# Two zero products instead of three, the first keys and queries on two queues, the cap behind them

## Chip, core and metric

The kernel runs on one core of one Trainium2 chip. The metric is the device time of one execution in microseconds (us), as the median of several runs. Engines are named as in the profile: PE (TensorE, the products; PEld its weight loads), ACT (ScalarE), DVE (VectorE), POOL (GpSimd) and SP (SyncE, which issues nearly all transfers).

## What is computed

Capped attention (4 batches, 12 heads, 448 positions, 64 values a head), followed by a gated feed-forward layer with a three-tap convolution over the positions:

```python
def _attn_ref(q, k, v, cap):
    scores = np.matmul(q, k.transpose(0, 1, 3, 2)) / np.sqrt(q.shape[-1])
    scores = cap * np.tanh(scores / cap)
    attn = np.exp(scores - np.max(scores, axis=-1, keepdims=True))
    attn = attn / (np.sum(attn, axis=-1, keepdims=True) + 1e-09)
    return np.matmul(attn, v)

def _moe_ref(x, w_in, conv_w, w_out):       # x: (4, 448, 768)
    h = np.maximum(x @ w_in, 0.0)           # (4, 448, 1024)
    ...                                     # conv_out: three taps of conv_w over the positions of h
    return h * (1 / (1 + np.exp(-conv_out))) @ w_out
```

## The kernel before

**Tiles.** Two heads lie together on the 128 partitions as a *pair*, six pairs a batch, 24 in all. `prepare` (L381) loads a pair's keys (`kr`, 128x512), queries (`qr`, 128x448) and values (`vr`, 128x512). `scores` (L420) multiplies a *unit* of 128 keys with all queries, for the two heads side by side on the two halves of the array: three units a pair, plus a rest unit (`spr`) with the last 64 keys of both heads. The first twelve pairs (`RAW`) use f32 operands, which the PE runs as two passes a product. A unit of scores stays in PSUM (`sp`, two buffers), ACT takes the tanh in place (L454, scaled by `tsc_sb`, a factor made from the cap by two DVE operations, L287 and L288) and then the exponential into SBUF (`E`, L458, scaled by `cap_sb`). `values` (L463) multiplies E with the values (`acc`); row sums come from products with ones (`sm`, L572, for the first pairs) or from sums on DVE (`P`). The result is copied out (`su`, `xu`), divided, split into two float parts (`x`) and fed to the feed-forward products `hps` and `ops`.

**Weights.** While the first pairs run, `weight_unit` (L307) turns 64-bit weights into two f32 parts. Each block is one operation on ACT (L322), three on DVE (L324 to L329), a cast to the high part (`wi_h`) and a subtraction (`wi_l`). The cast, as the copies `su`, `xu` and the cast `x`, is made by `either` (L246): it may run on ACT or on DVE.

**Order.** Every step is a `Task` with an engine, an assumed cost, a due time and its predecessors. `Plan.run` (L85) goes through them once, on the host, while the program is built: each engine takes, among the tasks that can start, the one due first, and an `either` task goes to the engine where it would end first by the assumed costs. So a change of a due time or a cost at the start can move later instructions, and can move a copy from one engine to the other. On the chip each engine works through its list in this fixed order.

**The start.** The plan gives these steps the earliest due times. SP loads the cap first (`t_cap`, L265, due -98: 4 bytes copied to each of 128 partitions), then the first pair's keys, queries and values (due -97, -97, -94), then the next ones. DVE fills `ones` and the padded tile `hp[0]` and the borders of two more (`consts`, L267). Then PE runs three products of `ones` with the zero tile (`warm`, L277), whose result nobody reads, and ACT takes an exponential of one column of it (`t_tab`, L284), which brings ACT's function table in. The first scores, on PE behind the warm products, need the first pair's keys and queries; the first tanh needs those scores and `tsc_sb`.

Of the kernel before, what the change touches and what calls it, by code (L numbers as in the profile page):

```python
# [10 lines left out]
ACTF = mybir.ActivationFunctionType  # L11
# [11 lines left out]
STEP = (9.5,) * 8 + (17.2,) * 16  # L23
FIRST = 6.0
DUE = {"w_in": (4.4, 57.93), "w_out": (63.06, 84.72), "prep": -5.0, "load": -34.0, "av": 5.0, "sum": 4.0,
       "x": 14.0, "x0": 14.0, "one": 4.5, "rec": 2.0, "ff": 27.0, "gate": -25.0, "wq": 6.0, "wld": -15.0}
AHEAD = {"w": 20.0, "qk": 40.0, "v": 36.0, "wld": 60.0}
BIAS, SWITCH = {"act": 1.0, "dve": 1.0}, 0.1
SLACK = {"pe": 0.0, "act": 0.1, "dve": 0.1, "sp": 0, "pool": 0}
# [7 lines left out]
HALF = 0.3755  # L37
COLD = (4.0, 0.4, 7.0)
SUMPE = 4
WARM = 3  # L40
LAND = 1.8
GBS = 300.0
RECIP = 2.95
# [129 lines left out]
def capped_attention_gated_mlp_kernel(  # L173
# [50 lines left out]
    plan = Plan({"sp": 2, "acc": 2, "m": 2, "su": 1, "cs": 1, "o": 2, **BUFS})  # L224
    task = plan.task
    ENGINE = {"sp": nc.sync, "pool": nc.gpsimd, "act": nc.scalar}
    ISSUE = {"sp": 0.65, "pool": 1.06, "act": 0.1}

    def f32(ap):
        return ap.bitcast(F32)  # L230
# [1 line left out]
    def dma(queue, nbytes, out, in_, due, deps, take=(), uses=(), after=0.0):  # L232
        def emit():
            a, b = out(), in_()
            ENGINE[queue].dma_start(out=a, in_=b)

        return task(queue, ISSUE[queue], emit, due, deps, take, uses, size=nbytes / (GBS * 1e3), after=after)

# [23 lines left out]
        return FIRST + sum(STEP[:p]) + (STEP[min(p, NP - 1)] * u)  # L262


    t_cap = dma("sp", 512, lambda: cap_sb, lambda: cap.to_broadcast([128, 1]), -98, ())  # L265

    def consts():  # L267
        nc.vector.memset(ones, 1.0)
        nc.vector.memset(ones[half[1], 64:96], 0.0)
        nc.vector.memset(ones[half[0], 96:128], 0.0)  # L270
        nc.vector.memset(hp[0], 0.0)
        for h in hp[1:]:
            nc.vector.memset(h[:, 0:1], 0.0)
            nc.vector.memset(h[:, S + 1:S + 2], 0.0)

    t_const = task("dve", 0.75, consts, -99)
    def warm():  # L277
        t = ps_m.tile([128, 512], F32, tag="m", name="warm")
        for _ in range(WARM):
            nc.tensor.matmul(out=t[:, 0:S], lhsT=ones, rhs=hp[0][:, 0:S], start=True, stop=True)  # L280

    if WARM:
        task("pe", 4.0 / 1.8, warm, -99, [t_const], [Buf("m")])
    t_tab = task("act", 0.1, lambda: nc.scalar.activation(out=eps_sb, in_=hp[0][:, 0:1], func=ACTF.Exp), -99, [t_const])  # L284

    def score_scale():
        nc.vector.reciprocal(out=tsc_sb, in_=cap_sb)  # L287
# [93 lines left out]
    def prepare(p):  # L381
        b, j = divmod(p, NPB)
        t0 = when(p)
        bq, bk, bs = Buf("q"), Buf("k"), Buf("s")
        b_v[p] = Buf("v")
        ld = t0 + DUE["load"] if p else -97
        lk = dma("sp", 128 * KW * 4, lambda: new(p, raw_p, "kr", [128, KW]), lambda: k[b, j], ld, (), [bk],
                 after=t0 - AHEAD["qk"])
        lq = dma("sp", 128 * S * 4, lambda: new(p, raw_p, "qr", [128, S]), lambda: q[b, j], ld, (), [bq],
                 after=t0 - AHEAD["qk"])  # L390
        t_v[p] = dma("sp", 128 * KW * 4, lambda: new(p, raw_p, "vr", [128, KW], bufs=BUFS["v"]), lambda: v[b, j], ld + 3, (),
                     [b_v[p]], after=t0 - AHEAD["v"])
        if p in RAW:
            prep[p], b_in[p] = [lk, lq], [bq, bk]
            return


        due = t0 + DUE["prep"]

        def q_hi():  # L400
            qs = new(p, raw_p, "qs", [128, 2, S], F32R, bufs=BUFS["s"])
            nc.vector.tensor_scalar(out=qs[:, 0], in0=T[p]["qr"], scalar1=tsc_sb[:, 0:1], scalar2=None, op0=ALU.mult)

        def q_lo():
            nc.vector.scalar_tensor_tensor(out=T[p]["qs"][:, 1], in0=T[p]["qr"], scalar=tsc_sb[:, 0:1],
                                           in1=f32(T[p]["qs"][:, 0]), op0=ALU.mult, op1=ALU.subtract)

        def k_hi(eng):
            copy(eng, new(p, raw_p, "ks", [128, 2, KW], F32R, bufs=BUFS["s"])[:, 0], T[p]["kr"])

        def k_lo():
            sub(T[p]["ks"][:, 1], T[p]["kr"], f32(T[p]["ks"][:, 0]))

        a = task("dve", dve(S, one=True, ptr=True), q_hi, due, [lq, t_tsc], [bs], [bq])
        a2 = task("dve", dve(S, ptr=True), q_lo, due + 0.3, [a], uses=[bq, bs])
        c = either(KW, k_hi, due + 0.1, [lk, a], uses=[bk, bs])
        c2 = task("dve", dve(KW), k_lo, due + 0.4, [c], uses=[bk, bs])
        prep[p], b_in[p] = [a, a2, c, c2], [bs]

    def scores(units, due):  # L420

        rest = units[0][1] == NU
        n = 1 if rest else 2
        out = [{} for _ in units]
        bufs = [Buf("m" if rest else "sp") for _ in units]

        def qk():
            for (p, u), sp in zip(units, out):
                if rest:
                    sp[0] = ps_m.tile([128, 512], F32, tag="m", name="spr").rearrange("p (a s) -> p a s", a=1)  # L430
                else:
                    sp[0] = ps_s.tile([128, 2, 512], F32, tag="sp", name="sp")
                X = T[p]
                if p in RAW:
                    parts = [(X["kr"], X["qr"])]
                else:
                    parts = [(X["ks"][:, w], X["qs"][:, l]) for w, l in ((0, 0), (0, 1), (1, 0))]
                for i, (w, x) in enumerate(parts):
                    for h in range(n):
                        r = slice(0, 128) if rest else half[h]  # L440
                        nc.tensor.matmul(out=sp[0][:, h, 0:S], lhsT=w[r, 128 * u:128 * u + 128], rhs=x[r],  # L441
                                         start=i == 0, stop=i == len(parts) - 1)

        cost = sum(2 * HALF if p in RAW else 3 * PASS for p, u in units)
        t_qk = task("pe", cost, qk, due, [t for p, u in units for t in prep[p]], bufs,
                    [b for p, u in units for b in b_in[p]], mode="full" if rest else "row")
        for (p, u), sp, bsp in zip(units, out, bufs):
            t_u = when(p, u / (NU + 1))
            raw = p in RAW
            b_e[p, u] = Buf("e")  # L450

            def tanh(sp=sp, raw=raw):
                x = sp[0][:, 0:n, 0:S]
                nc.scalar.activation(out=x, in_=x, func=ACTF.Tanh, **({"scale": tsc_sb[:, 0:1]} if raw else {}))  # L454

            def exp(p=p, u=u, sp=sp):
                E[p, u] = e_p.tile([128, 2, S], F32, tag="e", name="E")
                nc.scalar.activation(out=E[p, u][:, 0:n], in_=sp[0][:, 0:n, 0:S], func=ACTF.Exp, scale=cap_sb[:, 0:1])  # L458

            t = task("act", act(n * S, True, ptr=raw), tanh, t_u + 1, [t_qk, t_tsc], uses=[bsp])  # L460
            t_exp[p, u] = task("act", act(n * S, True, ptr=True), exp, t_u + 2, [t], [b_e[p, u]], [bsp], table="exp")
# [396 lines left out]
```

## Time and profile before

| | |
|---|---|
| median of 3 runs | 435.05 us (433.42 to 435.63) |
| the profiled execution, its own time | 434.71 us |
| its span, first to last instruction | 432.9 us |
| PE busy | 418.6 us (97%) |
| DVE busy | 309.9 us (72%) |
| ACT busy | 289.1 us (67%) |
| chain that ended last | PE 78%, ACT 11%, DVE 7%, issue 2%, DMA 2% |

The profiled execution's own time is 1.8 us above its span, and 0.34 us below the median of the runs. Busy shares are means over a kernel whose first part (attention of the first pairs, weights) and last part (feed-forward) load the engines quite differently, so the stretches have to be looked at one by one.

### The profile page before, as it was taken

The numbers are of one execution on the slowest core, as the hardware profiler recorded it, in microseconds if no ns is written. First come the engines' busy times: TensorE is split into PE (matmuls) and PEld (weight loads), VectorE is DVE, ScalarE is ACT, GpSimd is POOL, SyncE is SP. The second block draws the span as 40 slices with busy tenths as digits, with TensorE's granted clock in tenths as the row PEclk, the third lists the DMA queues.
The fourth block names the chain that finished last, engine by engine and source line by source line (L and its number), as shares of the span: only waits on it lengthen the run. The fifth ranks groups of instructions, "written<-read, shape, count | busy, mean of one in ns | idle before, by whom it ended". The sixth has DMA issues, their size and how long they took to land.

```text
span 432.9 us, 5890 instructions
## 1 busy us (share of the span) xinstructions
PE 418.6 (97%) x2106; PEld 288.1 (67%) x2106; DVE 309.9 (72%) x548; ACT 289.1 (67%) x412; POOL 0.2 (0%) x4
## 2 busy tenths in 40 slices
PE   7987889999999999999999999999999999999996
PEld 3222234457577676868667868668677787999995
DVE  1788899999999965589899773498899813166400
ACT  4999999988999665358888545368697811454411
POOL 0000000000000000000000000000000000000000
PEclk9999999999999999999999999999999999999999
DMA  7668557887556988650211762633000374500181
GB/s 273 217 225 263 182 181 234 274 244 254 206 161 200 345 292 263 229 210 5 70 28 44 224 225 90 202 130 120 24 2 0 131 251 148 183 0 2 30 336 53
DMA packets 37085, 70.90 MB, mean 164 GB/s; under 512 B 6336, under 2 KB 20160, under 8 KB 37056
## 3 DMA queue, kind: packets, MB, share of 16 engines
q1 hardware_dynamic: 37056, 70.53, 49.8%
q8 instruction: 17, 0.28, 0.3%
q14 instruction: 12, 0.10, 0.1%
HBM read 58.61 MB, written 11.84 MB: 163 GB/s over the span
## 4 chain that ended last, share of the span: by engine, by line
PE 78%; ACT 11%; DVE 7%; issue 2%; DMA 2%; ACTq 0%; DVEq 0%
PE ops L757 27%; PE hps L674 23%; PE acc L473 12%; PE sp L441 8%; ACT E L458 4%; ACT sp L454 4%; PE sm L631 2%; PE spr L441 2%; DVE P L489 1%; PE warm L280 1%; DMA kr<-in_k_dram 1%; DVE st_o L326 1%; ACT st_i L322 1%; DVE P L497 1%; DVE st_o L329 1%
## 5 line engine op out<-in xcount | busy, mean ns | idle before, releaser
L674 PE MATMUL hps<-x,wi_h 128*128 128x448 f32 x384 | 112.2, 373 | 0.0
L674 PEld LDWEIGHTS hps<-x,wi_h 128*128 128x128 f32 x384 | 70.8, 188 | 15.5 <-issue 6.7
L473 PE MATMUL acc<-E,vr 128*64 128x448 f32 x384 | 77.9, 546 | 0.0
L458 ACT ACTIVATE E<-sp,cap_sb 128x896 f32<-128x896 f32 x72 | 72.0, 1028 | 0.2
L674 PE MATMUL hps<-x,wi_l 128*128 128x448 f32 x192 | 70.2, 366 | 0.0
L700 DVE SCALAR_TENSOR_TENSOR ct<-hp,cw_sb,ct 128x448 f32<-128x448 f32 x64 | 43.1, 680 | 20.5 <-ACT ct L692 20.1
L473 PEld LDWEIGHTS acc<-E,vr 128*64 128x64 f32 x384 | 25.2, 136 | 44.3 <-issue 39.0
L636 DVE RECIPROCAL rb<-sm 128x448 f32<-128x448 f32 x12 | 35.5, 2956 | 16.4 <-PE sm L631 16.3
L757 PE MATMUL ops<-gh,wh 128*128 128x448 f32 x192 | 46.6, 372 | 0.3 <-ACT E L458 0.3
L757 PE MATMUL ops<-gh,wl 128*128 128x448 f32 x192 | 46.5, 367 | 0.0
L757 PE MATMUL ops<-gl,wh 128*128 128x448 f32 x192 | 43.8, 366 | 0.0
L441 PE MATMUL sp<-qr,kr 64*128 64x448 f32 x144 | 34.8, 582 | 8.7 <-ACT E L458 8.5
L253 ACT ACTIVATE osb<-ops 128x448 f32<-128x448 f32 x21 | 11.4, 544 | 46.6 <-PE ops L757 46.6
L757 PEld LDWEIGHTS ops<-gh,wh 128*128 128x128 f32 x192 | 35.3, 188 | 9.0 <-PE acc L473 1.4
L454 ACT ACTIVATE sp<-sp 128x896 f32<-128x896 f32 x36 | 31.0, 897 | 12.7 <-PE sp L441 12.6
L757 PEld LDWEIGHTS ops<-gh,wl 128*128 128x128 f32 x192 | 35.9, 188 | 4.1 <-DMA wh<-wo 0.7
L454 ACT ACTIVATE sp<-sp,tsc_sb 128x896 f32<-128x896 f32 x36 | 35.2, 1007 | 4.7 <-PE sp L441 4.7
L757 PEld LDWEIGHTS ops<-gl,wh 128*128 128x128 f32 x192 | 36.1, 188 | 3.1
L674 PEld LDWEIGHTS hps<-x,wi_l 128*128 128x128 f32 x192 | 36.1, 188 | 3.1
L441 PEld LDWEIGHTS sp<-qr,kr 64*128 64x128 f32 x144 | 11.8, 189 | 30.2 <-ACT E L458 18.1
L682 ACT ACTIVATE hp<-hps 128x448 f32<-128x448 f32 x32 | 17.4, 546 | 15.3 <-PE hps L674 13.0
L441 PE MATMUL sp<-qs,ks 64*128 64x448 f32 x216 | 26.9, 380 | 0.0
(84 smaller groups left out, 489.8 us busy)
## 6 DMA issues: line engine op xcount, KB each, us to landing
wh<-wo SPq DMA_DIRECT2D x24, 512.0 KB, 4.3
wl<-wo SPq DMA_DIRECT2D x24, 512.0 KB, 6.1
kr<-in_k_dram SPq DMA_DIRECT2D x24, 256.0 KB, 4.2
vr<-in_v_dram SPq DMA_DIRECT2D x24, 256.0 KB, 3.3
st_i<-in_moe_w_in_dram SPq DMA_DIRECT2D x12, 512.0 KB, 4.2
st_o<-in_moe_w_out_dram SPq DMA_DIRECT2D x24, 256.0 KB, 4.3
wo<-st_o SPq DMA_DIRECT2D x24, 256.0 KB, 3.6
qr<-in_q_dram SPq DMA_DIRECT2D x24, 224.0 KB, 4.3
```

What stands on the lines that cost most here:

```text
L253: nc.scalar.activation(out=out, in_=in_, func=ACTF.Copy)
L280: nc.tensor.matmul(out=t[:, 0:S], lhsT=ones, rhs=hp[0][:, 0:S], start=True, stop=True)
L441: nc.tensor.matmul(out=sp[0][:, h, 0:S], lhsT=w[r, 128 * u:128 * u + 128], rhs=x[r], start=i == 0, stop=i == len(parts) - 1)
L454: nc.scalar.activation(out=x, in_=x, func=ACTF.Tanh, **({"scale": tsc_sb[:, 0:1]} if raw else {}))
L458: nc.scalar.activation(out=E[p, u][:, 0:n], in_=sp[0][:, 0:n, 0:S], func=ACTF.Exp, scale=cap_sb[:, 0:1])
L473: nc.tensor.matmul(out=T[p]["acc"][half[h], 0:S], lhsT=T[p]["vr"][:, c:c + 64], rhs=E[p, u][:, 0 if u == NU else h, :], start=u == 0, stop ...
L631: nc.tensor.matmul(out=X["sm"][half[h], 0:S], lhsT=ones[:, 0:64], rhs=X["P"][:, h], start=True, stop=True)
L636: nc.vector.reciprocal(out=new(p, n_p, "rb", [128, S], bufs=BUFS["rb"]), in_=X["sm"][:, 0:S])
L674: nc.tensor.matmul(out=hps[0][:, 0:S], lhsT=w[:, c, ws], rhs=x[:, l, :], start=(c == 0 and i == 0), stop=(c == NCC - 1 and i == 2))
L682: t = task("act", act(S, True), lambda H=H, hps=hps: nc.scalar.activation(out=H[:, 1:S + 1], in_=hps[0][:, 0:S], func=ACTF.Relu), d - 10, ...
L700: nc.vector.scalar_tensor_tensor(out=ct[g][:, i], in0=H[:, o:o + S], scalar=cw_sb[:, f, o:o + 1], in1=ct[g][:, i], op0=ALU.mult, op1=ALU.add)
L757: nc.tensor.matmul(out=ops[0][:, 0:S], lhsT=W[part][:, f, :], rhs=G[l][:, f, :], start=(cnt["n"] == 0), stop=(cnt["n"] == 3 * NFC - 1))
```

## The change

- The zeroing of `hp[0]` becomes a task of its own (`t_zero`), the first on DVE. The warm products and `t_tab` wait for it alone, and the other constants come after it.
- The warm products are two in place of three, and their weights are `hp[0]` as well, in place of `ones`.
- The first pair's keys are loaded in two pieces: keys 0 to 127 (64 KB) first of all on SP, the other columns (192 KB) next. Its queries (224 KB) are issued by ACT, on ACT's own queue. The first unit of scores waits only for the first piece and the queries (`prep[p][0::2]`).
- The cap's load is due at -30 in place of -98, behind the first pair's values.
- The plan's assumed cost of a DMA issue on ACT is 0.6 in place of 0.1.

```diff
-WARM = 3
+WARM = 2
...
-    ISSUE = {"sp": 0.65, "pool": 1.06, "act": 0.1}
+    ISSUE = {"sp": 0.65, "pool": 1.06, "act": 0.6}
...
-    t_cap = dma("sp", 512, lambda: cap_sb, lambda: cap.to_broadcast([128, 1]), -98, ())
+    t_cap = dma("sp", 512, lambda: cap_sb, lambda: cap.to_broadcast([128, 1]), DUE["cap"], ())
+
+    def zeros():
+        nc.vector.memset(hp[0], 0.0)
...
-    t_const = task("dve", 0.75, consts, -99)
+    t_zero = task("dve", 0.35, zeros, -100)
+    t_const = task("dve", 0.6, consts, -99, [t_zero])
...
-            nc.tensor.matmul(out=t[:, 0:S], lhsT=ones, rhs=hp[0][:, 0:S], start=True, stop=True)
+            nc.tensor.matmul(out=t[:, 0:S], lhsT=hp[0][:, 0:128], rhs=hp[0][:, 0:S], start=True, stop=True)
...
-        task("pe", 4.0 / 1.8, warm, -99, [t_const], [Buf("m")])
+        task("pe", 1.6 * WARM / 1.8, warm, -99, [t_zero], [Buf("m")])
...
+            lk = [dma("sp", 128 * 128 * 4, lambda: new(p, raw_p, "kr", [128, KW])[:, 0:128], lambda: k[b, j, :, 0:128], -101, (),
+                      [bk])]
+            lq = dma("act", 128 * S * 4, lambda: new(p, raw_p, "qr", [128, S]), lambda: q[b, j], -101, (), [bq])
+            lk.append(dma("sp", 128 * (KW - 128) * 4, lambda: T[p]["kr"][:, 128:], lambda: k[b, j, :, 128:], -96, (), uses=[bk]))
...
-        t_qk = task("pe", cost, qk, due, [t for p, u in units for t in prep[p]], bufs,
+        t_qk = task("pe", cost, qk, due, [t for p, u in units for t in (prep[p] if p or u else prep[p][0::2])], bufs,
```

How the instructions move. On SP, at the program's start, before (the numbers behind the names tell tiles apart: `kr_113`, `qr_120` and `vr_122` are the first pair's):

```order
L235 DMA cap_sb_87<-in_cap_dram 128x1
L235 DMA kr_113<-in_k_dram 128x512
L235 DMA qr_120<-in_q_dram 128x448
L235 DMA vr_122<-in_v_dram 128x512
L235 DMA kr_124<-in_k_dram 128x512
L235 DMA qr_128<-in_q_dram 128x448
```

and in the changed kernel (`kr_107` and `vr_121` are the first pair's):

```order
L235 DMA kr_107<-in_k_dram 128x128
L235 DMA kr_107<-in_k_dram 128x384
L235 DMA vr_121<-in_v_dram 128x512
L235 DMA cap_sb_87<-in_cap_dram 128x1
L235 DMA kr_124<-in_k_dram 128x512
L235 DMA qr_126<-in_q_dram 128x448
```

The cap moves from the first place to the fourth, the keys become two transfers, and the first queries leave this queue.

On ACT, from the start to the second pair's first exponential, before (`st_i` is a block of `w_in`, or of the convolution's weights where it is 128x24):

```order
L297 ACTIVATE eps_sb_90<-eps_sb_90 128x1
L454 ACTIVATE sp_140<-sp_140,tsc_sb_88 128x2x448
...
L322 ACTIVATE st_i_100<-st_i_100 128x512
L454 ACTIVATE sp_155<-sp_155,tsc_sb_88 128x2x448
...
L458 ACTIVATE E_191<-spr_152,cap_sb_87 128x448
L253 ACTIVATE st_i_101<-st_i_101 128x24
L454 ACTIVATE sp_179<-sp_179,tsc_sb_88 128x2x448
L454 ACTIVATE sp_186<-sp_186,tsc_sb_88 128x2x448
L458 ACTIVATE E_219<-sp_179,cap_sb_87 128x896
```

and in the changed kernel:

```order
L235 DMA qr_104<-in_q_dram 128x448
...
L465 ACTIVATE sp_130<-sp_130,tsc_sb_88 128x2x448
L301 ACTIVATE eps_sb_90<-eps_sb_90 128x1
...
L465 ACTIVATE sp_155<-sp_155,tsc_sb_88 128x2x448
L326 ACTIVATE st_i_100<-st_i_100 128x512
...
L469 ACTIVATE E_187<-spr_147,cap_sb_87 128x448
L253 ACTIVATE wi_h_92<-st_i_100 128x512
L253 ACTIVATE st_i_101<-st_i_101 128x24
L465 ACTIVATE sp_169<-sp_169,tsc_sb_88 128x2x448
L465 ACTIVATE sp_193<-sp_193,tsc_sb_88 128x2x448
L253 ACTIVATE wi_h_92<-st_i_100 128x512
L469 ACTIVATE E_221<-sp_169,cap_sb_87 128x896
```

ACT begins with a transfer's issue, the small exponential `eps_sb` has moved behind the first tanh, the first weight block behind the third tanh, and two `wi_h` casts that DVE made before are now ACT's. Over the whole program ACT has two `wi_h` casts and one `x` cast more and two `su` copies and one `xu` copy fewer; on DVE it is the other way round. On PE the order differs in the first sixteen entries only (the second pair's units are spread between the first pair's values); on DVE, ACT and SP neighbours change places up to about the 180th, the 115th and the 38th entry.

## Rows read from the trace of the kernel before

**Rows 1.** Stretches of the span: busy us of each engine, granted clock, DMA share, GB/s.

```profile
0.00:8.00 8.00, 6.20 (x12) 2.67 (x14) 1.65 (x14) 1.69 (x3) 0.20 (x4) 1.00 0.70 226
8.00:61.50 53.50, 45.96 (x234) 14.47 (x230) 42.89 (x87) 52.61 (x76) 0.00 (x0) 1.00 0.69 226
61.50:110.00 48.50, 47.35 (x226) 26.15 (x228) 48.01 (x116) 43.41 (x68) 0.00 (x0) 1.00 0.80 252
110.00:433.00 323.00, 319.10 (x1642) 244.78 (x1640) 217.38 (x333) 191.43 (x267) 0.00 (x0) 1.00 0.42 139
```

**Rows 2.** Timeline of the first 9 us: start us, duration us, engine, line, operation.

```profile
0.73 0.39 SPq L235 DMA_DIRECT2D cap_sb<-in_cap_dram  x1
0.83 0.17 DVE L268 MEMSET ones<- 128x128 f32 x1 [0.83 <-PEq L847]
...
1.18 0.42 SPq L235 DMA_DIRECT2D kr<-in_k_dram  x1
...
1.31 0.43 DVE L271 MEMSET hp<- 128x450 f32 x1
...
1.80 4.85 PE L280 MATMUL warm<-hp,ones 128*128 128x448 f32 x6 [1.80 <-DVE hp L274]
...
2.12 0.43 SPq L235 DMA_DIRECT2D vr<-in_v_dram  x1
...
3.81 0.16 DVE L287 RECIPROCAL tsc_sb<-cap_sb 128x1 f32<-128x1 f32 x1 [2.03 <-DMA cap_sb<-in_cap_dram]
4.01 0.15 DVE L288 TENSOR_SCALAR tsc_sb<-tsc_sb 128x1 f32<-128x1 f32 x1
...
4.21 0.34 PEld L280 LDWEIGHTS warm<-hp,ones 128*128 128x128 f32 x1 [0.41 <-issue]
...
4.45 0.20 ACT L297 ACTIVATE eps_sb<-eps_sb 128x1 f32<-128x1 f32 x1 [2.23 <-DVE eps_sb L294]
...
4.95 0.34 PEld L280 LDWEIGHTS warm<-hp,ones 128*128 128x128 f32 x1 [0.41 <-issue]
...
6.58 0.51 PEld L441 LDWEIGHTS sp<-qr,kr 64*128 64x128 f32 x4 [1.29 <-issue]
6.58 2.22 PE L441 MATMUL sp<-qr,kr 64*128 64x448 f32 x8
...
8.11 0.98 ACT L454 ACTIVATE sp<-sp,tsc_sb 128x896 f32<-128x896 f32 x1 [3.45 <-PE sp L441]
```

**Rows 3.** DMA view of 2.0 to 2.5 us, first values: KB, us from issue to landing.

```profile
vr<-in_v_dram SPq DMA_DIRECT2D x1, 256.0 KB, 3.9
```

**Rows 4.** Instructions on the first queries, to 14 us: ns, minimum, median and maximum.

```profile
L441 PE MATMUL sp<-qr,kr x14: 536/558/1093, 6.6 to 13.9; 64*128 64x448 f32 x14
```

**Rows 5.** ACT from 8 to 61.5 us by line and shape: busy us, mean ns.

```profile
L458 ACT ACTIVATE E<-sp,cap_sb 128x896 f32<-128x896 f32 x19 | 19.6, 1067 | 0.0
...
L253 ACT ACTIVATE wi_h<-st_i 128x512 fp32r<-128x512 f32 x3 | 2.1, 698 | 0.0
L253 ACT ACTIVATE xu<-acc 128x448 f32<-128x448 f32 x3 | 1.9, 641 | 0.0
L253 ACT ACTIVATE su<-sm 128x448 f32<-128x448 f32 x3 | 1.7, 579 | 0.0
...
L253 ACT ACTIVATE x<-xu 128x448 fp32r<-128x448 f32 x1 | 0.6, 577 | 0.3 <-DVE xu L605 0.3
```

**Rows 6.** DVE from 13 to 61.5 us by line and shape; its waits, 8 to 61.5.

```profile
L251 DVE CAST wi_h<-st_i 128x512 fp32r<-128x512 f32 x9 | 3.8, 424 | 0.1
...
L251 DVE COPY xu<-acc 128x448 f32<-128x448 f32 x2 | 1.2, 622 | 0.0
...
L251 DVE CAST x<-xu 128x448 fp32r<-128x448 f32 x2 | 0.7, 342 | 0.0
...
DVE st_i L324 <- ACT st_i L322: 11.3, 4, 8.0
DVE wi_l L256 <- ACT wi_h L253: 0.9, 1, 0.9
```

More of the change, by code (lines that the diff above doesn't have):

```diff
@@ L25 @@
 DUE = {"w_in": (4.4, 57.93), "w_out": (63.06, 84.72), "prep": -5.0, "load": -34.0, "av": 5.0, "sum": 4.0,
-       "x": 14.0, "x0": 14.0, "one": 4.5, "rec": 2.0, "ff": 27.0, "gate": -25.0, "wq": 6.0, "wld": -15.0}
+       "x": 14.0, "x0": 14.0, "one": 4.5, "rec": 2.0, "ff": 27.0, "gate": -25.0, "cap": -30.0, "wq": 6.0, "wld": -15.0}
 AHEAD = {"w": 20.0, "qk": 40.0, "v": 36.0, "wld": 60.0}
@@ L270, in consts @@
         nc.vector.memset(ones[half[0], 96:128], 0.0)
-        nc.vector.memset(hp[0], 0.0)
         for h in hp[1:]:
@@ L279, in warm @@
         for _ in range(WARM):
-            nc.tensor.matmul(out=t[:, 0:S], lhsT=ones, rhs=hp[0][:, 0:S], start=True, stop=True)
+            nc.tensor.matmul(out=t[:, 0:S], lhsT=hp[0][:, 0:128], rhs=hp[0][:, 0:S], start=True, stop=True)
     if WARM:
-        task("pe", 4.0 / 1.8, warm, -99, [t_const], [Buf("m")])
-    t_tab = task("act", 0.1, lambda: nc.scalar.activation(out=eps_sb, in_=hp[0][:, 0:1], func=ACTF.Exp), -99, [t_const])
+        task("pe", 1.6 * WARM / 1.8, warm, -99, [t_zero], [Buf("m")])
+    t_tab = task("act", 0.1, lambda: nc.scalar.activation(out=eps_sb, in_=hp[0][:, 0:1], func=ACTF.Exp), -99, [t_zero])
     def score_scale():
@@ L386, in prepare @@
         ld = t0 + DUE["load"] if p else -97
[L387 to L390, printed above, removed]
+        if p:
+            lk = [dma("sp", 128 * KW * 4, lambda: new(p, raw_p, "kr", [128, KW]), lambda: k[b, j], ld, (), [bk],
+                      after=t0 - AHEAD["qk"])]
+            lq = dma("sp", 128 * S * 4, lambda: new(p, raw_p, "qr", [128, S]), lambda: q[b, j], ld, (), [bq],
+                     after=t0 - AHEAD["qk"])
+        else:
+            lk = [dma("sp", 128 * 128 * 4, lambda: new(p, raw_p, "kr", [128, KW])[:, 0:128], lambda: k[b, j, :, 0:128], -101, (),
+                      [bk])]
+            lq = dma("act", 128 * S * 4, lambda: new(p, raw_p, "qr", [128, S]), lambda: q[b, j], -101, (), [bq])
+            lk.append(dma("sp", 128 * (KW - 128) * 4, lambda: T[p]["kr"][:, 128:], lambda: k[b, j, :, 128:], -96, (), uses=[bk]))
         t_v[p] = dma("sp", 128 * KW * 4, lambda: new(p, raw_p, "vr", [128, KW], bufs=BUFS["v"]), lambda: v[b, j], ld + 3, (),
@@ L393, in prepare @@
         if p in RAW:
-            prep[p], b_in[p] = [lk, lq], [bq, bk]
+            prep[p], b_in[p] = [*lk, lq], [bq, bk]
             return
@@ L415, in prepare @@
         a2 = task("dve", dve(S, ptr=True), q_lo, due + 0.3, [a], uses=[bq, bs])
-        c = either(KW, k_hi, due + 0.1, [lk, a], uses=[bk, bs])
+        c = either(KW, k_hi, due + 0.1, [*lk, a], uses=[bk, bs])
         c2 = task("dve", dve(KW), k_lo, due + 0.4, [c], uses=[bk, bs])
```

## The prediction

> **What bounds the kernel now.** The stretches of the span come first [rows 1]. From 110 us to the end PE is busy 319.1 of 323.0 us: that part has a fixed length, and whatever enters it earlier ends earlier by as much. Between 61.5 and 110 us DVE is full (48.01 of 48.50 us) and PE nearly so (47.35). From 8 to 61.5 us ACT is the full engine (52.61 of 53.50 us), while PE is idle for 7.5 us of it and DVE for 10.6. In the first 8 us nothing is full but PE, and PE's 6.2 busy us are mostly products of zeros. So the kernel is a relay: PE's zero products, ACT's first stage, a stretch in which DVE and PE share the limit, and PE's long last part. The change touches the first leg alone; the question is how much of its gain the second and third legs pass on.
>
> The timeline shows the first leg [rows 2]. DVE fills the constants from 0.83 us. The zero products run from 1.80 to 6.65 us, and the first scores' weights are loaded at 6.58, directly behind them. The first tanh starts at 8.11 us, after ACT waited 3.45 us for those scores. The data were not what PE waited for: the values, the third transfer of the queue behind keys and queries, were issued at 2.12 us and took 3.9 us to land [rows 3], so they were there at 6.02 us, and the keys and queries ahead of them no later. Nor was the cap: DVE took it up at 3.81 and had the factor for tanh ready at 4.16 us [rows 2]. Three products of zeros alone held the scores back.
>
> **The change, step by step.**
>
> *Zero tile first.* It is now DVE's first operation: 0.83 + 0.43 = 1.26 us. With the few hundredths that lay between DVE's last constant and PE's start, the zero products begin at 1.29 in place of 1.80 us: 0.51 us earlier. The ones are wanted by the row sums, long after; they cost nothing.
>
> *Two products in place of three.* A product is two passes, and the loads at 4.21 and 4.95 us are 0.745 us apart [rows 2], so two passes less are 1.49 us. From the first load to the first scores' load six passes took 6.58 - 1.80 = 4.78 us; four take 3.29. The first scores can load at 1.29 + 3.29 = 4.58 us, 2.00 us earlier.
>
> *The first scores at the lower clock.* The profile's granted clock reads 1.00 (2.4 GHz) from the start [rows 1], but the durations do not agree in the first microseconds: the same product on the first queries takes 1093 ns at most and 558 ns at the median [rows 4], the ratio of the two levels, 2.4 and 1.2 GHz. The rise fell within the first scores before. Now they start 2 us sooner, and I let them run wholly at the lower level. From their load to the first tanh they took 8.11 - 6.58 = 1.53 us. Two passes at the lower level are 1.49, and the zero products show 4.85 - 6 x 0.745 = 0.38 us of run-out, with 0.03 to ACT's start: 1.90 us. First tanh at 6.48, that is 1.63 us earlier. If the clock came up as early in them as before, it would be 2.00.
>
> *First keys and queries.* Both now leave at about 0.73 us, the time of the first issue. The nearest row is the values' 3.9 us [rows 3] with 480 KB and the cap ahead of them: landing at 4.63 us. The other bound is the cap's own 3.81 - 0.73 = 3.08 us: 3.81. Now 288 KB are wanted, with pieces of the other queue between them. At the far end PE waits 0.05 us; I take none. If the cover were gone (the queries at 5.5, say), each tenth would be a tenth lost.
>
> *The cap, fourth in the queue.* Issues are 0.47 us apart (1.18 to 2.12 for two), so it leaves at 0.73 + 3 x 0.47 = 2.14 us. Ahead of it are 64 + 192 + 256 KB on SP and the queries' 224 on ACT's queue: 736 KB, just what the values' landing at 6.02 us stood for before (256 + 224 + 256), which had the cap in front. So I expect the cap at about 6.0 and the factor 0.35 us later, at 6.4: a hair before the scores at 6.48. Bounds: 2.14 + 3.08 = 5.2 us if it passes as alone; 6.02 + 3.08 = 9.1 if it begins only when the values are there. This term eats the upside (a first tanh at 6.1 would wait for the factor), and its far end is a rival below. Behind the factor on DVE wait only small operations on the cap. SP issues four transfers ahead of the second pair's, as before, so those leave when they did.
>
> *ACT's list.* The queries' issue and the table load lie before the first tanh, in ACT's 3.45 us of waiting: nothing. The small exponential moves behind the first tanh, into ACT's full stretch: 0.20 us [rows 2]. The first weight block goes behind a third tanh. The two casts that ACT takes over at once wait for DVE's steps on the same blocks; the nearest wait on such a cast is 0.9 us [rows 6], so two cost between 0 and 1.8. I take 0.5, near the low end, because two tanh stand between the two casts and give DVE 2 us. Up to the 19th wide exponential, the last before 61.5 us, ACT's order holds two wi_h and two x casts more, two su and one xu copy fewer: 2 x 0.698 + 2 x 0.577 - 2 x 0.579 - 0.641 = 0.75 us more [rows 5]; one x cast is only moved forward, so that later 0.17 is left. ACT thus passes 61.5 us earlier by 1.63 - 0.20 - 0.50 - 0.75 = 0.2, and is 0.76 us ahead soon after.
>
> *DVE's list.* It is the mirror: three copies of 0.62 more, casts of 2 x 0.424 + 0.342 less: 0.67 us more [rows 6]. Its first weight block comes earlier by 1.63 - 0.20 - 0.98 (the third tanh) = 0.45 us. Up to 61.5 us DVE waited 11.3 us for ACT's weight blocks, 8.0 of it at the start, so 3.3 us of later waits can take the surplus up; after 61.5 there is no room. What DVE gains lies between -0.2 and 1.5 us.
>
> *Sum.* ACT brings 0.76 us, DVE about as much, PE's waits in the shared stretch (1.15 us) are small enough to pass it on, and the last part keeps it. I take 0.75 us: 434.71 - 0.75 = 433.96 for an execution like the profiled one, which stands 0.34 us below the median of the runs; so **434.3 us** as a median.
>
> **The rivals.**
>
> *All of it comes through.* First tanh 2.0 us earlier, and DVE's waits swallow the moved copies. For it: 3.3 us of such waits, and no engine but ACT is full up to 61.5 us. Against it: the factor's 6.4 us, and ACT's added 0.95 us. It gives 435.05 - 2.0 = 433.05 us.
>
> *Nothing comes through.* DVE, full from 61.5 to 110 us, has 0.67 us more and starts only 0.45 sooner; PE then enters its last part when it did. It gives 435.05 us. A part is lost where two queues are no faster than one. The Trainium skill (DMA: Bandwidth & Descriptors, Issuing engines are not separate DMA queues) says that transfers of different issuers run on the same 16 engines and that issuing from several saves only the issuing time. No row here has two queues. By that rule the queries would land as one queue brings them, and with one issue's 0.47 us not saved the sum would fall from 0.75 to 0.28 us.
>
> *Slower: the cap takes the place of the zero products.* If its 128 small pieces get their turn only when the values are down, it lands at up to 9.1 us and the first tanh starts at 9.1 + 0.35 = 9.45, 1.34 us later than before; with 0.95 us more on ACT that is 2.3 us: 437.35. The point from which it decides is a landing at 6.1 us; from 7.75 the start is no gain at all. Against it: the values, with two transfers ahead, took only 0.8 us longer than the cap alone, so transfers overlap.
>
> *Slower: the clock stays low.* With two products PE could fall idle before the scores, if the data were late. The Trainium skill (TensorE: Matmul & The Clock Gate, What's actually happening) has the throttled clock as the default, which sustained activity releases; by that rule a shorter run of zeros speaks against the change. Here PE has work from 1.29 us on in both bounds, so I expect the rise near where it was. Each microsecond at 1.2 GHz costs half a microsecond of products; 6 us of it, 3 us less 0.75: 437.3.
>
> **How the numbers follow.** My forecast has 0.50, all of it 0.20, nothing 0.22, the cap 0.05, the clock 0.03. A measurement of this kernel can tell about 0.5% from no change, 2.2 us: below 432.9 or above 437.2. Faster by that is somewhat under half of the second case and a small tail of the forecast: 0.15. Slower is a good half of the last two: 0.05. The rest, 0.80, is within. The range takes in the forecast with its bounds (0.2 to 1.6 us), the case of nothing with the scatter of the runs, and most of the second: 432.4 to 436.0 us.
>
> **What would show it.** In the changed profile: zero products from about 1.3 to 4.9 us; the scores' load at 4.6; the factor's reciprocal (DVE) at about 6.0; the first tanh at 6.5. A first tanh later than 6.7 with the scores done is the cap; scores' loads later than 4.7 are the queries; first products still above 900 ns behind 9 us are the clock. On ACT, two casts with short waits near 15 to 18 us. The 19th wide exponential should come 0 to 0.5 us earlier, and PE's long last part begin 0.75 us earlier. The forecast is wrong if the start gains its 1.6 us and the last part does not move, or moves by all of it.

## The result, and the profile after

The changed kernel takes **438.02 us** (median of 11 runs, 435.70 to 440.13), the kernel before on the same chip 434.66: a ratio of 1.0078 [1.0059, 1.0096], slower by 0.8%. The forecast was 434.3 us and its range ended at 436.0. The profiled execution took 438.5 us, its span is 436.6. Five runs of this document stand far off, one of e2 (2335 us) and four of the kernel before (688 to 2340 us); they are left out of the ratios and the counts of runs, but not of the medians, which they move by less than 0.2 us.

The mean granted clock of each run splits the runs in two. Four of the eleven have 0.998 or more and a median of 435.89 us; seven have 0.991 to 0.996 and a median of 439.17. The kernel before ran 92 times beside the experiments, those far-off runs aside, always with 0.998 or more. The page of the changed kernel shows such a fall in its row of clocks (40 slices of the span, tenths of 2.4 GHz):

```profile
PEclk9989999999999999999999999999999999999999
```

The same stretches as in [rows 1], and then the one where the clock fell (columns as there):

```profile
0.00:8.00 8.00, 6.31 (x14) 2.36 (x14) 1.15 (x11) 1.49 (x2) 0.20 (x4) 1.00 0.71 168
8.00:61.50 53.50, 45.07 (x223) 14.37 (x224) 40.25 (x85) 51.14 (x75) 0.00 (x0) 0.97 0.68 225
61.50:110.00 48.50, 45.68 (x217) 24.34 (x217) 47.13 (x114) 41.55 (x65) 0.00 (x0) 1.00 0.76 234
110.00:433.00 323.00, 321.98 (x1653) 246.53 (x1651) 221.06 (x341) 194.44 (x271) 0.00 (x0) 1.00 0.44 142
...
24.60:30.40 5.80, 5.72 (x20) 1.76 (x20) 3.90 (x9) 5.26 (x8) 0.00 (x0) 0.71 0.37 126
```

Between 8 and 61.5 us DVE has done 2.64 us less than before (40.25 of 42.89) and ACT 1.47 less. Between 24.6 and 30.4 us the granted clock is 0.71: PE is busy, but for a good half of the time at 1.2 GHz. At (1 - 0.71) x 5.8 this costs 1.7 us.

The timeline of the start, to be read against [rows 2] (start, duration, engine, line):

```profile
0.72 0.39 ACTq L235 DMA_DIRECT2D qr<-in_q_dram  x1
0.73 0.89 SPq L235 DMA_DIRECT2D kr<-in_k_dram  x2
1.38 3.35 PE L284 MATMUL warm<-hp 128*128 128x448 f32 x4 [1.38 <-DVE hp L268]
2.14 0.43 SPq L235 DMA_DIRECT2D cap_sb<-in_cap_dram  x1
4.67 0.51 PEld L452 LDWEIGHTS sp<-qr,kr 64*128 64x128 f32 x4 [1.29 <-issue]
4.67 2.08 PE L452 MATMUL sp<-qr,kr 64*128 64x448 f32 x8
7.59 0.16 DVE L291 RECIPROCAL tsc_sb<-cap_sb 128x1 f32<-128x1 f32 x1 [5.79 <-DMA cap_sb<-in_cap_dram]
8.04 0.98 ACT L465 ACTIVATE sp<-sp,tsc_sb 128x896 f32<-128x896 f32 x1 [5.39 <-DVE eps_sb L297]
10.12 1.02 PE L452 MATMUL sp<-qr,kr 64*128 64x448 f32 x4 [2.42 <-ACT E L469]
```

The scores start at 4.67 us, as forecast (4.58). But DVE can take up the cap only at 7.59, not at 6.0, and the first tanh starts at 8.04 in place of 8.11: all but 0.07 us of the 1.9 us that the scores gained is lost in a wait for the cap (the row of the tanh names `eps_sb`, the next small operation on the cap in DVE's list). Meanwhile PE, which has done its scores, waits 2.42 us at 10.1. The chain of waits now begins with the cap (start, us):

```profile
2.14 5.43 DMA cap_sb<-in_cap_dram
```

So the start gives next to nothing here, and what makes the kernel slower than before lies behind it. Two views of 14 to 26 us show where: PE, and ACT (whose second row is the exponential that PE waits for).

```profile
20.59 1.77 PE L452 MATMUL sp<-qr,kr 64*128 64x448 f32 x8
24.68 1.02 PE L452 MATMUL sp<-qr,kr 64*128 64x448 f32 x4 [2.31 <-ACT E L469]
```

```profile
18.28 0.63 ACT L253 ACTIVATE wi_h<-st_i 128x512 fp32r<-128x512 f32 x1
...
23.59 1.03 ACT L469 ACTIVATE E<-sp,cap_sb 128x896 f32<-128x896 f32 x1
```

PE has done its ready work at 22.4 us and waits 2.31 us for that exponential. Before, the same place reads:

```profile
23.72 1.02 PE L441 MATMUL sp<-qr,kr 64*128 64x448 f32 x4 [1.58 <-ACT E L458]
```

with its exponential on ACT:

```profile
22.59 1.08 ACT L458 ACTIVATE E<-sp,cap_sb 128x896 f32<-128x896 f32 x1
```

From first tanh to this exponential ACT takes 14.48 us before and 15.55 in the changed order: two casts `wi_h` in place of one, the later small exponential and a rest unit's tanh that moved forward. The clock falls right behind the wait of 2.31 us. The wait of 2.42 us at 10.1 us passed in this execution without a fall.

### The profile page after: what moved, and what is told of

Same layout as the page of the kernel before. It is cut to its first block, busy times and chain, and to the rows that moved or that the text cites. A ratio compares the mean times of both kernels' runs of the same rounds, so it can differ in the third digit from the quotient of the medians.

```text
span 436.6 us, 5876 instructions
## 1 busy us (share of the span) xinstructions
PE 419.1 (96%) x2104; PEld 287.6 (66%) x2104; DVE 309.6 (71%) x548; ACT 289.2 (66%) x412; POOL 0.2 (0%) x4
## 4 chain that ended last, share of the span: by engine, by line
PE 78%; DVE 7%; ACT 6%; DMA 5%; issue 2%; SPq 1%; ACTq 0%; DVEq 0%
PE ops L768 27%; PE hps L685 23%; PE acc L484 13%; PE sp L452 8%; ACT E L469 2%; PE sm L642 2%; PE spr L452 2%; ACT sp L465 2%; DMA st_o<-in_moe_w_out_dram 2%; DMA cap_sb<-in_cap_dram 1%; PE sm L583 1%; DVE st_o L330 1%; DMA r_d<-rr 1%; DVE st_o L333 1%; DVE ct L711 1%
## 5 line engine op out<-in xcount | busy, mean ns | idle before, releaser
L484 PE MATMUL acc<-E,vr 128*64 128x448 f32 x384 | 79.8, 556 | 0.0
```

Of the source, the lines that this page charges most:

```text
L484: nc.tensor.matmul(out=T[p]["acc"][half[h], 0:S], lhsT=T[p]["vr"][:, c:c + 64], rhs=E[p, u][:, 0 if u == NU else h, :], start=u == 0, stop ...
```

## The experiments

**Theory A**: the cap, fourth, lands late and takes the start's gain; the new order alone costs the rest, through longer waits of PE, behind which the clock falls. **Theory B**: two zero products and the idle PE at the start are the cause; the order is harmless. **Theory C**: the cap behind the values delays the second pair's loads. "Clock up" means a mean granted clock of 0.998 or more; ratios are to the kernel before on the same chip (medians 434.53, 434.64 and 434.58 in the three groups).

| kernel | median us | ratio | runs, clock up | median, clock up |
|---|---|---|---|---|
| changed kernel | 438.02 | 1.0078 [1.0059, 1.0096] | 11, 4 | 435.89 |
| e1: start alone | 435.99 | 1.0042 [1.0024, 1.0059] | 12, 8 | 435.5 |
| e2: start, cap first | 433.54 | 0.9979 [0.9967, 0.9991] | 11, 11 | 433.5 |
| e3: change, cap first | 435.93 | 1.0025 [1.0004, 1.0046] | 12, 4 | 433.9 |
| e4: order alone | 436.64 | 1.0045 [1.0021, 1.0070] | 8, 4 | 435.55 |
| e5: e3, one wait filled | 435.00 | 1.0019 [1.0003, 1.0036] | 12, 8 | 434.4 |
| e6: e2, no cap load | 433.31 | 0.9979 [0.9968, 0.9989] | 11, 11 | 433.3 |
| e7: e2, three products | 433.96 | 0.9992 [0.9982, 1.0002] | 12, 12 | 434.0 |
| e8: e2, one queue | 434.16 | 0.9987 [0.9975, 1.0000] | 12, 12 | 434.2 |
| e9: e3, two waits filled | 435.25 | 1.0002 [0.9990, 1.0015] | 12, 12 | 435.25 |
| e10: e2, cap on POOL | 433.93 | 0.9992 [0.9980, 1.0003] | 12, 12 | 433.9 |
| e11: e2, one delay | 436.16 | 1.0031 [1.0015, 1.0046] | 6, 1 | 434.84 |
| e12: e11, wait filled | 434.80 | 1.0013 [1.0002, 1.0023] | 11, 11 | 434.8 |

### Start, order and cap apart (e1 to e4)

e1 has the order of before with the new start; the loads are issued inside the old tasks, so that the plan does not move. e2 is the same with the cap left in the first place.

```diff
-            nc.tensor.matmul(out=t[:, 0:S], lhsT=ones, rhs=hp[0][:, 0:S], start=True, stop=True)
+            nc.tensor.matmul(out=t[:, 0:S], lhsT=hp[0][:, 0:128], rhs=hp[0][:, 0:S], start=True, stop=True)
...
+                nc.sync.dma_start(out=kr[:, 0:128], in_=k[b, j, :, 0:128])
+                nc.scalar.dma_start(out=new(p, raw_p, "qr", [128, S]), in_=q[b, j])
...
+            lq.emit = lambda: nc.sync.dma_start(out=T[p]["kr"][:, 128:], in_=k[b, j, :, 128:])
```

and in e1 alone

```diff
+            def values_cap(load=t_v[p].emit):
+                load()
+                nc.sync.dma_start(out=cap_sb, in_=cap.to_broadcast([128, 1]))
```

> The order of before, instruction by instruction, with the changed start alone (zero tile first, two zero products, keys in two pieces, queries on ACT's queue, cap fourth on SP). Theory A (the cap's late landing takes the start's gain, and the new order costs the rest): the factor for tanh at about 7.9 us, the small exponential ahead of the first tanh waits for the cap too, so the first tanh at 8.0 to 8.7 us; time 434 to 435.7 us, no drop of the granted clock. Theory B (the shorter run of zero products and PE's idle time behind it are the cause, the order is harmless): 437 to 439 us, as the changed kernel. Theory C (the cap fourth delays the second pair's loads, and these cost later): first tanh as in A, but ACT waits again before 20 us and the time is 436 to 437 us.

> As the first of this call, but the cap stays the first transfer on SP. Theory A: the cap lands at about 3.8 us, the first scores are loaded at 4.7 to 5.2 us, first tanh 6.5 to 7.0 us; the gain goes through ACT's full stretch: 433.0 to 433.8 us, which beats before. Theory B: two zero products as in the changed kernel, so 437 to 439 us. Theory C: as A.

The chain of e1, its first tanh and one row of its PE, then e2's start:

```profile
2.14 6.16 DMA cap_sb<-in_cap_dram
...
9.07 0.96 ACT L469 ACTIVATE sp<-sp,tsc_sb 128x896 f32<-128x896 f32 x1
...
11.13 1.60 PE L456 MATMUL sp<-qr,kr 64*128 64x448 f32 x4 [3.74 <-ACT E L473]
```

```profile
4.19 0.16 DVE L287 RECIPROCAL tsc_sb<-cap_sb 128x1 f32<-128x1 f32 x1 [2.40 <-DMA cap_sb<-in_cap_dram]
...
4.76 1.77 PE L449 MATMUL sp<-qr,kr 64*128 64x448 f32 x8
...
5.82 0.98 ACT L462 ACTIVATE sp<-sp,tsc_sb 128x896 f32<-128x896 f32 x1 [0.79 <-PE sp L449]
```

e1 is slower than before without any change of order: its first tanh comes at 9.07 us, since the cap took 6.16. With the cap first, the same start is faster than before, with the first tanh at 5.82 and no clock lost. The two differ in one issue, and that issue is worth 435.99 - 433.54 = 2.4 us. e1 missed what Theory A expected of it: its time lies above 435.7 us, and four of its runs lost the clock, in the profile behind the wait of 3.74 us. Theory B falls: e2 has two products, and its clock is up in all runs. An idle PE at the start does cost e1 its clock in some runs, but there the late cap keeps PE idle, and not the shorter run of zeros.

e3 is the changed kernel with the cap first; e4 is the changed order with the start of before.

```diff
+            def cap_first(load=lk[0].emit):
+                nc.sync.dma_start(out=cap_sb, in_=cap.to_broadcast([128, 1]))
+                load()
```

```diff
+            def old_loads():
+                nc.sync.dma_start(out=cap_sb, in_=cap.to_broadcast([128, 1]))
+                nc.sync.dma_start(out=new(p, raw_p, "kr", [128, KW]), in_=k[b, j])
+                nc.sync.dma_start(out=new(p, raw_p, "qr", [128, S]), in_=q[b, j])
```

> The changed kernel with its order, but the cap issued first on SP. Theory A: first tanh 6.6 to 7.1 us, but the new order keeps its cost: 435.5 to 437.5 us, with the same long waits of PE for the exponential near 22 to 25 us and the clock's drops in some runs. If the cap alone were the cause: 433 to 434 us. Theory B: 437 to 439 us.

> The changed kernel's order with the start of before (cap first, keys whole, queries on SP, three products of ones with zeros, ones filled first). Theory A: first tanh at 8.1 us as before, and the order costs by itself: 436.5 to 439 us, with runs below a mean granted clock of 0.998 among them. Theory B (the start is the cause): 434.3 to 435.3 us, as before.

PE's longest wait is 2.30 us in e3 and 2.32 in e4; the clock falls behind it in e3's profile, and in e4's behind a later one of 1.92:

```profile
22.88 1.86 PE L458 MATMUL sp<-qr,kr 64*128 64x448 f32 x4 [2.30 <-ACT E L475]
```

```profile
23.38 1.02 PE L460 MATMUL sp<-qr,kr 64*128 64x448 f32 x4 [2.32 <-ACT E L477]
...
61.54 1.02 PE L460 MATMUL sp<-qr,kr 64*128 64x448 f32 x4 [1.92 <-ACT E L477]
```

The four add up: new start -0.21% (e2), new order +0.45% (e4) or +0.46 (e3 over e2), cap fourth +0.63 (e1 over e2) or +0.53 (changed kernel over e3). With the clock up the new order costs only 433.9 - 433.5 = 0.4 us; that rests on four runs of e3. By e4's four it is 435.55 - 434.53 = 1.0 us, and e9 below, the new order with two waits filled and the clock up in all twelve runs, stands 435.25 - 433.54 = 1.7 us above e2. So the order costs something without any fall of the clock, between 0.4 and 1.7 us, and these runs do not settle how much; the rest of its price is the clock. A trace shows the same: in the profile of e5, also the new order, the clock holds to 61 us and the first tanh comes at 5.63 us, yet the 18th and 19th wide exponentials start 1.7 us later than in e2 (e2, then e5):

```profile
58.30 1.99 ACT L466 ACTIVATE E<-sp,cap_sb 128x896 f32<-128x896 f32 x2
```

```profile
60.01 1.90 ACT L480 ACTIVATE E<-sp,cap_sb 128x896 f32<-128x896 f32 x2
```

The cap costs 435.5 - 433.5 = 2.0 us with the clock up. Theory C finds no support: up to 61.5 us PE waits in e1 and in the changed kernel for nothing but the zero tile and ACT's exponentials, and the first tanh waited for the operations on the cap.

### The parts of the start (e6, e7, e8, e10)

Each changes one thing of e2. e6 leaves out the cap's load and fills the tile with a constant:

```diff
+        nc.vector.memset(cap_sb, 30.0)
...
+    t_cap.emit = lambda: None
```

> The kernel with the order of before and the new start, cap first (433.54 us), without the cap's transfer: the tile is filled on DVE with the constant 30 (the kernel leaves out reading the cap). It prices the 128 small pieces. If they hold up the transfers behind them: the dip to 13 to 62 GB/s between 2 and 3.5 us is gone, the scores' weights still load at about 4.6 to 4.7 (the zero products set that), so the median falls by 0 to 0.5 us: 433.0 to 433.6. If the dip is only the time any first transfer takes: it stays, and the time is 433.3 to 433.8.

DMA share and GB/s (last two columns) near 3 us, in e2 and then in e6:

```profile
2.00:2.50 0.50, 0.50 (x2) 0.21 (x1) 0.00 (x0) 0.49 (x2) 0.00 (x0) 1.00 0.30 83
2.50:3.00 0.50, 0.50 (x1) 0.13 (x1) 0.00 (x0) 0.16 (x1) 0.00 (x0) 1.00 0.64 174
3.00:3.50 0.50, 0.50 (x2) 0.34 (x1) 0.00 (x0) 0.00 (x0) 0.00 (x0) 1.00 1.05 218
```

```profile
2.00:2.50 0.50, 0.50 (x2) 0.21 (x1) 0.15 (x1) 0.49 (x2) 0.00 (x0) 1.00 0.66 179
2.50:3.00 0.50, 0.50 (x1) 0.12 (x1) 0.28 (x2) 0.16 (x1) 0.00 (x0) 1.00 1.09 401
```

e6's loads leave one issue earlier, 0.45 us; shifted by that, 174 and 218 GB/s stand against 179 and 401: with the cap's 512 bytes in the way about half is moved for half a microsecond. (The dip of 13 to 62 GB/s that the expectation names is the kernel before's.) But e6 has a dip of its own soon after, with no cap in it, and its first values take longer to land than e2's, which have the cap ahead of them. e6's window, then the first values in e2 and in e6 (KB, us from issue to landing):

```profile
4.00:4.50 0.50, 0.50 (x1) 0.00 (x0) 0.00 (x0) 0.00 (x0) 0.00 (x0) 1.00 0.74 152
```

```profile
vr<-in_v_dram SPq DMA_DIRECT2D x1, 256.0 KB, 3.7
```

```profile
vr<-in_v_dram SPq DMA_DIRECT2D x1, 256.0 KB, 4.9
```

So the small pieces are not shown to be what slows the loads. The end sees nothing of it (0.9979 both times): the scores' load, behind the zero products, hardly moves (4.76 and 4.66 us). With the cap behind the values the rate falls further, and there the first tanh waits. A window of the changed kernel:

```profile
6.00:6.50 0.50, 0.50 (x4) 0.02 (x2) 0.00 (x0) 0.00 (x0) 0.00 (x0) 1.00 0.37 35
```

The values ahead of the cap are late there too. A later issue of SP waits for their landing (waits of SP's queue: us in total, times, longest; then that issue):

```profile
SPq L235 <- DMA vr<-in_v_dram: 1.6, 1, 1.6
```

```profile
7.39 0.80 SPq L235 DMA_DIRECT2D st_i<-in_moe_w_in_dram  x2
```

So the values were down at about 7.4 us, and the cap at 7.57, only 0.2 us behind them.

e7 has the third product again (`range(3)`), e8 issues the queries on SP:

```diff
-                nc.scalar.dma_start(out=new(p, raw_p, "qr", [128, S]), in_=q[b, j])
+                nc.sync.dma_start(out=new(p, raw_p, "qr", [128, S]), in_=q[b, j])
```

> The kernel with the order of before and the new start, cap first (433.54 us, first tanh at 5.82 us), with three products of zeros again. Theory A (the third product is start time and no more): scores' weights load at 6.0 to 6.2 us, the first tanh at 7.0 to 7.6, median 434.0 to 434.6. Rival B (two products are worse for the clock, three would give something back): the first scores run shorter passes and the median is 433.6 or less.

> The kernel with the order of before and the new start, cap first (433.54 us, scores' weights loaded at 4.73 us), with the first queries on SP's queue again, behind the first 128 keys. It prices the second queue. If a second queue saves only an issue's 0.47 us: the scores' weights load at 4.7 to 5.2 us and the median is 433.5 to 434.0. If two queues carry more at once: the load comes later than 5.5 and the median is 434.2 or more.

PE in e7, then in e8:

```profile
1.38 4.26 PE L280 MATMUL warm<-hp 128*128 128x448 f32 x6 [1.38 <-DVE hp L268]
5.57 1.77 PE L449 MATMUL sp<-qr,kr 64*128 64x448 f32 x8
```

```profile
4.67 2.77 PE L449 MATMUL sp<-qr,kr 64*128 64x448 f32 x8
...
6.58 0.98 ACT L462 ACTIVATE sp<-sp,tsc_sb 128x896 f32<-128x896 f32 x1 [2.42 <-PE sp L449]
```

The third product costs 0.4 us (433.96 against 433.54; the intervals of the two ratios overlap), less than the 1.49 us of two passes at the lower clock: in e7 the rise came within the zero products, so they took 4.26 us and not 4.85 as in [rows 2], and the scores load at 5.57, earlier than expected. In e8 the queries are there when PE wants them, so the second queue saves nothing that this row shows: e8's ratio, 0.9987, has an interval that overlaps e2's, and its median, 434.16, lies just above the expected 433.5 to 434.0. Its scores ran wholly at 1.2 GHz (2.77 us against 1.77 in e2), so the time at which the clock first rises varies between executions: these scores differ by 1.0 us.

e10 gives the cap a queue of its own, POOL's:

```diff
+    t_cap.emit = lambda: nc.gpsimd.dma_start(out=cap_sb, in_=cap.to_broadcast([128, 1]))
```

> The kernel with the order of before and the new start (433.54 us with the cap first on SP), with the cap issued by POOL at the start, on a queue of its own, so that keys and queries are first on theirs. If the cap's 128 pieces are slow only where transfers were queued before them: the factor is ready by 4.5 us, the scores' weights load at 4.7, and the median is 433.2 to 433.8. If they are slow wherever large transfers run beside them: the cap takes more than 5 us from its issue, the first tanh is later than 6.3 us and the median 434.2 or more, with PE waits over 2 us and falls of the clock.

```profile
1.22 0.66 POOL L266 DMA_DIRECT2D cap_sb<-in_cap_dram  x1 [0.78 <-POOLq L856]
...
6.44 0.16 DVE L288 RECIPROCAL tsc_sb<-cap_sb 128x1 f32<-128x1 f32 x1 [4.63 <-DMA cap_sb<-in_cap_dram]
```

Nothing stands ahead of the cap on its queue, and still it takes 6.44 - 1.22 = 5.2 us. From issue to DVE's taking up it took 2.58 us in e8 (first, the whole of the loads behind it on one queue), 3.08 before and 3.46 in e2 (the queries beside it on another queue). With large loads issued before it, it took 5.2 here, 5.45 in the changed kernel and 6.18 in e1. So its time went with its place among the issues. How much of the 5.2 us is due to POOL's queue is open, since the DMA view lists that queue as of another kind, and its 32 packets are not the transfer that SP makes (0 to 8 us: packets, MB, share of 16 engines):

```profile
q0 software_dynamic: 32, 0.00, 0.3%
```

The first values took 6.1 us to land here, with no cap on their queue. The Trainium skill (DMA: Bandwidth & Descriptors, Queues, rings and completion order) has each DMA engine take turns between the queues, packet by packet; by that rule a queue of its own should have brought the cap sooner, and the 5.2 us do not show it, nor, on a queue of another kind, do they refute it. The clock held here although PE waited 1.85 us at 9.25, so the second expectation is right in the cap's time and wrong in the wait, the clock and the median.

### The waits and the clock (e5, e9, e11, e12)

e5 is e3 with two zero products on PE in the wait at 22.9 us, into a tile that is overwritten later; e9 adds the same ahead of the seventh pair's second unit, `(6, 1)`.

```diff
+                if (p, u) == (2, 1):
+                    T[1]["acc"] = ps_a.tile([128, 512], F32, tag="acc", name="acc")
+                    for _ in range(2):
+                        nc.tensor.matmul(out=T[1]["acc"][:, 0:S], lhsT=hp[0][:, 0:128], rhs=hp[0][:, 0:S],
+                                         start=True, stop=True)
```

> The changed kernel with the cap loaded first (as in the earlier run of that kind, 435.93 us, 8 of 12 runs with a mean clock under 0.998), and two more products of zeros, whose result is overwritten, on PE just ahead of the third pair's second unit, where PE waited 2.30 us for a wide exponential. Theory A (the new order costs time through that wait, behind which the clock falls): the wait is cut to under 1 us, nearly all runs have a clock of 0.998 or more, median 433.7 to 434.5. Rival B (the falls have nothing to do with that wait, or come from the rest of the order): half of the runs or more stay under 0.998, median 435.5 to 436.5. Rival C (the two products only push PE's work back): clock up, but the median above 435.

> The changed kernel with the cap first and two products of zeros at each of two places: ahead of the third pair's second unit (as in the run before, 435.00 us, 4 of 12 runs under a clock of 0.998, where the profiled run lost its clock at 61 us behind a PE wait of 1.83 us) and ahead of the seventh pair's second unit, where that wait is. Theory A (each of PE's waits of 1.8 us and more is a place where the clock may fall): the waits are cut to under 1.2 us, all or all but one run at 0.998 or more, median 433.9 to 434.5. Rival B (the falls move on to some other place, or come by chance): 3 or more runs stay under, median 434.8 to 436.

In e5's profile the clock holds at 22.9 us, where the wait is now 0.64, and falls at the next long one:

```profile
22.99 1.02 PE L463 MATMUL sp<-qr,kr 64*128 64x448 f32 x4 [0.64 <-ACT E L480]
...
61.07 1.02 PE L463 MATMUL sp<-qr,kr 64*128 64x448 f32 x4 [1.83 <-ACT E L480]
...
60.00:65.00 5.00, 3.93 (x14) 1.46 (x16) 4.94 (x12) 5.00 (x9) 0.00 (x0) 0.74 0.62 199
```

Falls go from 8 of 12 runs (e3) to 4 (one wait filled) to none (both filled). The medians are not what was expected, though. e5's, 435.00, lies above the 433.7 to 434.5 of Theory A. In e9 five runs lie between 433.66 and 434.34 us, seven between 435.17 and 435.75, with the clock up in all. What parts them stays open; the profiled execution, of the upper group, ran its first scores at the lower clock and had its first tanh at 6.58 us, 0.8 later than e2's. That alone does not explain it: e5's profile, with the first tanh 0.95 us sooner, has its 18th and 19th wide exponentials at 60.01 us, e9's has them at 59.81. Nor do the two products push PE's work back, the third possibility of e5's expectation: in e9's profile PE still waits 0.59 us behind the first pair, and behind the second it goes on at 60.88 us, about when the 18th of these exponentials ends.

e11 makes such a wait in e2, where there was none; e12 fills it.

```diff
+                if (p, u) == (1, 2):
+                    nc.scalar.activation(out=sp[0][:, 0:n, 0:S], in_=sp[0][:, 0:n, 0:S], func=ACTF.Copy)
```

> The kernel with the order of before and the new start, cap first (433.54 us, 11 of 11 runs at a clock of 0.998 or more, PE's longest wait 1.56 us at 21.7), with ACT copying the second pair's third unit onto itself just ahead of its exponential, some 0.97 us of ACT work that delays this one exponential, for which PE waits. Theory A (a PE wait of over 2 us lets the clock fall, whatever made it): PE's wait grows to about 2.5 us, a third or more of the runs fall under 0.998, median 435 to 437; runs with the clock up at 434.2 to 434.8. Rival B (the falls belong to the new order, not to the wait): all runs at 0.998 or more, 434.2 to 434.8.

> The same delayed exponential, with two products of zeros on PE in the wait that it makes, ahead of the third pair's second unit. ACT's delay is the same; only PE's idle time is filled. Theory A: all or all but one run at 0.998 or more, median 434.2 to 434.8. Rival B' (it is the delay itself, or ACT's later work, that costs): like the run without the fill, within 0.3 us.

PE and the stretch behind the wait in e11, then PE in e12:

```profile
23.66 1.03 PE L449 MATMUL sp<-qr,kr 64*128 64x448 f32 x4 [2.53 <-ACT E L468]
24.62 4.87 PE L483 MATMUL acc<-E,vr 128*64 128x448 f32 x16
...
23.60:30.00 6.40, 6.34 (x28) 2.11 (x32) 4.05 (x9) 6.31 (x10) 0.00 (x0) 0.73 0.42 143
```

```profile
20.41 1.77 PE L440 MATMUL acc<-hp 128*128 128x448 f32 x4
22.99 1.02 PE L454 MATMUL sp<-qr,kr 64*128 64x448 f32 x4 [0.81 <-ACT E L473]
23.94 3.23 PE L488 MATMUL acc<-E,vr 128*64 128x448 f32 x16
```

One delayed exponential, nothing else, and the clock falls in 5 of 6 runs; the sixteen products behind the wait take 4.87 us instead of 3.23. With the same delay and the wait filled it falls in none of 11. That is one half of Theory A shown from both sides: such a wait lets the clock fall, and the new order makes one (2.30 and 2.32 us in e3 and e4, at most 1.56 in e2). It is not all that the new order costs, as e9 shows. The delay itself, with the wait filled, costs 434.80 - 433.54 = 1.3 us, the fall another 1.4.

## Why the prediction was wrong

- **Zero tile first, two products: right.** 1.38 and 4.67 us measured, 1.29 and 4.58 forecast.
- **The first scores at the lower clock: right as a bound.** Where they ran wholly at 1.2 GHz (e8), load to tanh took 6.58 - 4.67 = 1.91 us, forecast 1.90. In e2 it took 1.06, since the clock rose earlier.
- **First keys and queries: right.** No row of the changed kernel has PE waiting for them. The prediction cited the Trainium skill (DMA: Bandwidth & Descriptors, Issuing engines are not separate DMA queues) for a saving of an issue at most; e8 shows no larger one.
- **"The cap, fourth in the queue": failed.** The step said that 736 KB ahead of it are "just what the values' landing at 6.02 us stood for", and put the landing at 6.0. It landed at 7.57 (2.14 + 5.43). What failed is the landing time carried over from before, when the cap stood first: the values themselves were down only at about 7.4 us, and the cap 0.2 behind them. The first values took 3.9 us before and 3.7 in e2, but 4.9 in e6 without a cap's load and 6.1 in e10, so the cap's small pieces are not the only reason; in e1 the values were down at 6.6 us, when SP's issue that waits for them goes out, and the cap 1.7 us later, so the pieces can add to it. Why the loads are slower in the new start without the cap in front stays open. The text held a late cap as a rival at 0.05, with 7.75 us as the point from which the start gains nothing, and 7.57 is next to it; but the argument against it ("transfers overlap") was taken from a cap that had nothing ahead of it.
- **"ACT's list": the size about right, the consequence missed.** Up to the exponential at 23.6 us ACT had 1.07 us more, against 0.95 forecast for the whole leg and 0.5 for waits. DVE's list was not measured by itself. With the clock up the order costs 0.4 to 1.7 us (e3, e4, e9). The prediction asked what ACT and DVE could take up and never whom ACT's surplus keeps waiting: PE, whose wait of 1.58 us became 2.31.
- **The rival of the clock: the right engine, the wrong place.** It looked for the loss in the first microseconds, for want of zero products. All runs of e2, with two products, keep the clock. In the profiled run of the changed kernel it falls behind a wait in the middle, and in e1's behind the wait that the late cap makes. The Trainium skill (TensorE: Matmul & The Clock Gate, What's actually happening) names the lower clock as the state that PE returns to without activity; e11 (0.73 behind a wait of 2.53 us) and e12 (the wait filled, no fall in 11 runs) agree.
- **The sum.** With the cap first, the order of before and the clock up, the start does bring 434.53 - 433.54 = 1.0 us, against 0.75 forecast for all. The late cap took that and 1 us more and the order 0.4 by e3's four runs, which makes the 435.9 us of the changed kernel's runs with the clock up; the clock took 2 to 4 us more in 7 of 11 runs. That the two slower rivals, 437.35 and 437.3 us, lie near the measured 438.02 is luck: the first tanh came at 8.04 us and not at 9.45, and the clock fell in the middle and not at the start.

## What to carry to other kernels

A tiny load that is spread over all partitions belongs in front of the large ones, or off the path altogether: its bytes say nothing about its landing. When a planner moves work between engines, compare PE's longest single wait before and after, not only the sums of busy time, and read the clock of every run and not of the profiled one alone. e2, the new start without the new order and with the cap first, beats both kernels (433.54 us, 0.9979 [0.9967, 0.9991]), though only by 0.2% of the kernel before. Two idle products in an unavoidable wait were a cheap remedy against the fall of the clock (436.16 to 434.80 us from e11 to e12), not against the rest of the order's price (e9).

## What the hardware showed that was not expected

Where PE had a single wait of 2.3 to 2.5 us, the clock fell in half of the runs or more (7 of 11 of the changed kernel, which has two such waits, 8 of 12 of e3, 4 of 8 of e4, 5 of 6 of e11), and in none of the 23 runs in which the waits were filled (e9, e12). The length alone does not decide: in single profiles 2.42 us (changed kernel, at 10.1 us), 2.32 (e4) and 1.85 us (e10) passed without a fall, 1.83 (e5) and 1.92 us (e4) were followed by one, and e1, with a wait of 3.74 us in its profile, lost the clock in 4 of 12 runs only. Such a fall costs 1.4 to 2.3 us at the end (434.8 to 436.3 in e11, 435.5 to 437.4 in e1, 433.9 to 436.2 in e3). And 512 bytes took 2.6 to 3.5 us from issue to use as the first load issued and 5.2 to 6.2 us with large loads issued before them; the rate of all transfers fell to 35 GB/s in the changed kernel (6.0 to 6.5 us).
